# Re-pricing a static scheduler: new durations, a turn cost between 64 and 128 rows, and an offset per kind of step

## The chip, the cores and the metric

The kernel runs on one core of a Trainium2 chip. The metric is the device time of one execution in microseconds (us). Five engines work side by side, each through its own queue in program order: TensorE (PE, matmuls; its weight loads are PEld), VectorE (DVE), ScalarE (ACT), GpSimd (POOL), and SyncE (SP), which here issues all DMAs.

## The reference, cut to what matters

Linear attention with an exponential feature map, and then two MLPs over the same 2304 tokens, in 32-bit floats:

```python
def phi(x):                                   # x: 4 x 8 heads x 576 x 64
    proj = einsum('bhsd,df->bhsf', x, w_phi)  # f = 128
    proj = proj - max(abs(proj), axis=-1, keepdims=True)
    return concatenate([exp(proj), exp(-proj)], axis=-1)
q_p, k_p = phi(q), phi(k)
kv  = einsum('bhsf,bhsd->bhfd', k_p, v)
z   = sum(k_p, axis=2)
num = einsum('bhsf,bhfd->bhsd', q_p, kv)
den = einsum('bhsf,bhf->bhs', q_p, z)[..., None] + 1e-06
x   = (num / den) as 2304 x 512
x   = elu(x @ w_in) @ w_out                   # 512 -> 2048 -> 512
x   = (h * clip(h + 3, 0, 6) / 6) @ w2_out    # h = x @ w2_in
```

## The kernel before

The attention part is eight **units**, each of two heads over two batches. A unit is a set of steps, named by two letters and made by `add` in `unit` (from L250 on). In the order of their dependence they are:

- LD (SP): loads of raw k, q and v. Only unit 0 loads k and q in two pieces each (`LDk0`, `LDk1`, `LDq0`, `LDq1`).
- PJ (TensorE, L314): projections, matmuls of 64 rows, in three groups: all of k but the ninth block, the two ninth blocks ("x8"), all of q but the ninth block; unit 0 has five smaller groups. They write four banks of PSUM, the ring "p".
- MX and SB (DVE, L324 and L338): the largest absolute value, and the shift by it. SB releases the bank.
- EX (ACT, L347 and L354): both exponentials of k. KV (TensorE, L372): the sums of k times v, 72 matmuls of 128 rows and 130 columns in a unit, into the bank "a0" or "a1". ST (ACT, L390 and L392) copies them out.
- QT (TensorE, L397 and L403): transposes of shifted q into a bank of the ring "t", which has two. QE (ACT, L410 and L419): both exponentials of them. QT8 and QE8 are those of the ninth block.
- NM (TensorE, L431): numerator and denominator, into a bank of "t"; it needs ST and QE. NS (ACT, L446 and L450): copies of both out of the bank.
- RT, RV, RB (DVE, L455, L461, L469): transpose, reciprocal, transpose; MU (POOL, L478): the product, which is the MLPs' input.

A 32-bit matmul of the attention part stands in the trace as two instructions.

The MLP part works on groups of four 128-wide slices of the hidden layer over five blocks of tokens (four of 512 and one of 256). A step `hid` (L746) is 12 matmuls into a bank "p"; then come `act1` (ACT, L759, L760 or L762), `gate` (DVE, L773), `gate_hi` (ACT, L781), `gate_lo` (DVE, L788), and `outp` (L807), 12 matmuls into the banks "a0", "a1", "t0", "t1". Each 32-bit operand is split into a high and a low part, of which three products are taken. Weights come as 64-bit floats and are turned into 32-bit ones by eight integer steps on DVE (L675, L683, L687) and one on POOL (L692), and are split by two more on POOL (L714, L720). There are 32 weight pairs ("w"), each of two halves, in six slots. The first four slots exist from the start, so the weights of the first group are converted beside the attention part.

No order is written out. Every step states its engine, a duration, what it comes after (`after`: when that has ended; `behind`: when that has started), the buffers that it takes and a **rank**. `in_order` (L48) then plays the whole program through: at each turn it computes for each engine the soonest start of every ready step, keeps the steps within `WINDOW` of the soonest, and takes of these the one with the lowest rank. The queues of all engines, SP's and POOL's included, are issued in the order of the starts that it finds. A unit's step has the rank `u * PERIOD - tail`, where `tail` is the longest chain of durations from it to the unit's end. The MLP steps have the rank of a clock that starts at 8 times `PERIOD` and runs on by the matmuls' durations. A weight's steps have the rank of its first use less `W_LEAD`; in the first group they are spread over the units (`lead`).

Of the kernel before, what the change touches and what calls it, by code (L numbers as in the profile page):

```python
# [18 lines left out]
M1_GROUPS, M2_GROUPS = (4, 4, 4, 4), (4, 4, 4, 4)  # L19


PB, TB = 4, 2
KB, QB, KPB, EB, NSB, MXB, WB, GB = 3, 6, 3, 4, 2, 6, 4, 2
PERIOD, PROJ, TURN = 22.0, 0.225, 0.4
W_LEAD = 60.0


class Token:


    def __init__(self, ring):
        self.ring, self.users = ring, []


class Step:
    def __init__(self, engine, us, fn, after=(), rank=0.0, takes=(), uses=(), port=False, behind=()):
        self.engine, self.us, self.fn, self.rank, self.port = engine, us, fn, rank, port
        self.after, self.behind, self.takes = list(after), list(behind), list(takes)
        for t in uses:
            t.users.append(self)  # L40
        self.start = self.end = None


LATENCY = {"PE": 0.22, "DVE": 0.10, "ACT": 0.12, "POOL": 0.12, "SP": 2.2, "NONE": 0.0}
WINDOW = 0.06


def in_order(steps, rings):  # L48

    taken = {r: [] for r in rings}  # L50
    free = {e: 0.0 for e in LATENCY}
    port = 0.0
    waits, heirs = {}, {}
    for s in steps:
        need = {id(x): x for x in s.after + s.behind}
        waits[id(s)] = len(need)
        for x in need.values():
            heirs.setdefault(id(x), []).append(s)
    ready = {e: [s for s in steps if s.engine == e and not waits[id(s)]] for e in LATENCY}
    out = []  # L60

    def soonest(s):
        t = max([0.0] + [x.end + LATENCY[x.engine] for x in s.after] + [x.start for x in s.behind])
        extra = {}
        for k in s.takes:
            had = taken[k.ring]
            at = len(had) + extra.get(k.ring, 0) - rings[k.ring]
            extra[k.ring] = extra.get(k.ring, 0) + 1
            if at < 0:
                continue  # L70
            if at >= len(had):
                return None
            for x in had[at].users:
                if x.end is None:
                    return None
                t = max(t, x.end + LATENCY[x.engine])
        return t

    known = {}
    while len(out) < len(steps):  # L80
        best = None
        for e, some in ready.items():
            est = []
            for s in some:
                t = soonest(s)
                if t is not None:
                    t = max(t, free[e])
                    if s.port or e == "POOL":
                        t = max(t, port)
                    est.append((t, s))  # L90
            if est:
                t0 = min(t for t, _ in est)
                t, s = min(((t, s) for t, s in est if t <= t0 + WINDOW), key=lambda x: (x[1].rank, x[0]))
                if best is None or t < best[0]:
                    best = (t, s)
        if best is None:
            raise RuntimeError(f"no step can go on: {[(x.engine, x.rank, x.fn) for e in ready.values() for x in e][:40]}")
        t, s = best
        s.start, s.end = t, t + s.us
        if s.engine != "NONE":  # L100
            free[s.engine] = s.end
        if s.port or s.engine == "POOL":
            port = s.end
        for k in s.takes:
            taken[k.ring].append(k)
        ready[s.engine].remove(s)
        for x in heirs.get(id(s), ()):
            waits[id(x)] -= 1
            if not waits[id(x)]:
                ready[x.engine].append(x)  # L110
        out.append(s)
    order = sorted(range(len(out)), key=lambda i: (out[i].start, i))
    return [out[i] for i in order]
# [5 lines left out]


def pe1(n):
    return n / 2280 + 0.006


def dve(n):
# [1 line left out]


def act(n):
    return n / 1200 + 0.105  # L130


def pool(n, two=True):
# [4 lines left out]
def attention_then_two_mlps(  # L138
# [32 lines left out]
    R = S // 64  # L171
# [78 lines left out]
    def unit(u):  # L250
# [3 lines left out]
        def add(name, engine, us, fn, after=(), stage=None, **kw):  # L254

            s = step(engine, us, fn, after=[S_[x] for x in after], **kw)
            S_[name] = s
            if stage:
                s.behind += last.get((u - 1, stage), [])
                last.setdefault((u, stage), []).append(s)  # L260
            return s
# [22 lines left out]
        if u == 0:  # L284
            add("LDk0", "SP", 1.2, lambda: load("k", 0, 512), takes=[Tk["k"]], rank=-9)
            add("LDw", "SP", 0.6, lambda: nc.sync.dma_start(out=wphi, in_=w_phi), rank=-8)
            add("LDq0", "SP", 1.2, lambda: load("q", 0, 512), takes=[Tk["q"]], rank=-7)
            add("LDk1", "SP", 1.6, lambda: load("k", 512, R * 128), after=["LDk0"], rank=-6)
            add("LDq1", "SP", 1.6, lambda: load("q", 512, R * 128), after=["LDq0"], rank=-5)
            add("LDv", "SP", 1.6, load_v, takes=[Tk["v"]], rank=-4)  # L290
            ld = {("k", 0): ["LDk0", "LDw"], ("k", 1): ["LDk1"], ("q", 0): ["LDq0"], ("q", 1): ["LDq1"]}
        else:
            for s_ in "kq":
                add("LD" + s_, "SP", 2.8, bind_(load, s_, 0, R * 128), takes=[Tk[s_]], rank=(u - 1) * PERIOD, stage="LD")
            add("LDv", "SP", 1.6, load_v, takes=[Tk["v"]], rank=(u - 1) * PERIOD, stage="LD")
            ld = {(s_, i): ["LD" + s_] for s_ in "kq" for i in range(2)}
# [188 lines left out]
        for js in runs if u == 0 else (("k0", "k1"), ("x8",), ("q0", "q1")):  # L485
            items = [x for j in js for x in ITEMS[j]]
            tp = {(j, h): take("p") for j in js for h in range(2)}
            need = sorted({x for s_, r in items for x in ld[s_, int(r >= 4)]})
            pj = "PJ" + js[0]
            add(pj, "PE", len(items) * PROJ + TURN, bind_(projs, js), after=need, stage="PJ", takes=list(tp.values()),  # L490
                uses=[Tk[x] for x in sorted({s_ for s_, _ in items})])
            if js == ("x8",):
                Tk["sh8"] = take("sh8")
            for j in js:
                n = len(ITEMS[j]) * NF
                for h in range(2):
                    tm, ts = take("mx"), Tk["sh8"] if j == "x8" else take({"k": "shk", "q": "shq"}[j[0]])
                    add(f"MX{j}{h}", "DVE", dve(n), bind_(peak, j, h), after=[pj], takes=[tm],
                        uses=[tp[j, h]], stage="MX")
                    add(f"SB{j}{h}", "DVE", dve(n), bind_(shift, j, h), after=[f"MX{j}{h}"], stage="SB",  # L500
                        takes=[] if j == "x8" and h else [ts], uses=[tp[j, h], tm])
                    Tk["sh", j, h] = ts
# [18 lines left out]
                    S_[f"KV{j}{h}"].behind.append(S_[f"KVk0{h}"])  # L521
        for h in range(2):
            t = Tk["st", h] = take(f"st{h}")
            add(f"ST{h}", "ACT", act(260) + act(252), bind_(stat, h), after=[f"KV{j}{h}" for j in ("k0", "k1", "x8")],
                takes=[t], uses=[Tk["acc", h]], stage="ST")
        for c in range(2):
            for h in range(2):
# [1 line left out]
                Tk["e", h, c] = te  # L529
                add(f"QT{h}{c}", "PE", 4 * 0.109, bind_(q_tr, h, c), after=[f"SBq{c}{h}"], takes=[t],  # L530
                    uses=[Tk["sh", f"q{c}", h]], stage="QT")
                add(f"QE{h}{c}", "ACT", 2 * act(512), bind_(q_exp, h, c), after=[f"QT{h}{c}"], takes=[te],
                    uses=[t], stage="QE")
        t = take("t")
        add("QT8", "PE", 2 * 0.109, q_tr8, after=["SBx80", "SBx81"], takes=[t], uses=[Tk["sh8"]], stage="QT")
        add("QE8", "ACT", 4 * act(128), q_exp8, after=["QT8"], uses=[t], stage="QE")
        S_["QT8"].behind += [S_["QT01"], S_["QT11"]]
        S_["QE8"].behind += [S_["QE01"], S_["QE11"]]
        before = None
        for c in range(2):  # L540
            n = 64 * (4 + c)
            for bb in range(2):
                tn = take("nsd")
                for h in range(2):
# [1 line left out]
                    add(f"NM{h}{c}{bb}", "PE", 2 * pe4(n), bind_(num, h, c, bb),  # L546
                        after=[f"ST{h}", f"QE{h}{c}"] + ["QE8"] * c, takes=[t],
                        uses=[Tk["st", h], Tk["e", h, c]], stage="NM")
                    add(f"NS{h}{c}{bb}", "ACT", 2 * act(n) + 0.05, bind_(num_out, h, c, bb), after=[f"NM{h}{c}{bb}"],
                        takes=[tn] if h == 0 else [], uses=[t], stage="NS")  # L550
                    if before:
                        S_[f"NM{h}{c}{bb}"].behind.append(before)
# [14 lines left out]
            for x in s.after:  # L567
                tail[id(x)] = max(tail.get(id(x), 0.0), tail[id(s)] + LATENCY[x.engine])
        for s in mine:
            s.rank = u * PERIOD - tail[id(s)]  # L570
        for name, s in S_.items():
            (a_users if name[:2] in ("LD", "PJ", "MX", "SB", "EX", "KV") else b_users).append(s)
            if name[:2] == "SB":
# [272 lines left out]
    for w in range(2 * FT):  # L846
        j = w % len(SLOT)
        WT[w] = Token(f"w{j}")
        for i in range(2):
            lead = max(first[w] - W_LEAD, (2 * w + i + 1) * PERIOD / 1.2 if w < GROUPS[0][1] else 0.0)  # L850
            ts_, ta, tb = Token("s"), Token("ca"), Token("cb")
            x = step("SP", 1.4, bind_(fetch, w, i), takes=[ts_], rank=lead - 5, behind=[chain] if chain else [])
            chain = x
            cost = [0.6, 0.33, 0.33, 0.5, 0.6, 0.6, 0.6, 0.45]
            fns = to_f32(w, i)
            for n_, (us, fn) in enumerate(zip(cost, fns)):
                x = step(
# [150 lines left out]
```

## Time and profile before

| what | value |
|---|---|
| time, median of 3 runs | 1005.57 us (1004.29 to 1007.49) |
| profiled execution, time | 1007.1 us |
| its span in the trace | 1005.3 us |
| matmuls | 5312 |
| busy: TensorE, DVE, ACT, POOL | 986.8, 718.1, 422.7, 280.4 us |
| granted clock of TensorE, mean | 0.997 |

The span runs from the first to the last instruction of the profiled execution; its time holds 1.8 us more. Engines work at the same time, so the busy times don't add up to the span. Records of matmuls overlap each other by their pipelined ends: the distance between starts tells what a matmul costs, not its length.

### The profile page before, as it was taken

The page shows a single profiled execution, that of the slowest core. Times are in us where ns is not written, and L with a number is a line of the kernel's source. Part 1 is how long each engine was busy: PE and PEld are TensorE (multiplying, and loading weights), DVE is VectorE, ACT ScalarE, POOL GpSimd, SP SyncE. Part 2 cuts the span into 40 slices and gives each one's busy share as a digit, 9 for nine tenths or more (in the row PEclk, how much of TensorE's full clock was granted, in tenths as well). Part 3 has the DMA queues.
Part 4 walks back from the last instruction along what each step waited for, and adds up shares of the span by engine and source line. Part 5 has one row for each costly group of instructions (what it writes and reads, how often), then busy time and mean ns, then how long its engine had stood idle before and what let it go on. Part 6 is the DMA issues. An engine that isn't in the chain of part 4 may idle for free.

```text
span 1005.3 us, 13762 instructions
## 1 busy us (share of the span) xinstructions
PE 986.8 (98%) x5312; PEld 829.9 (83%) x5312; DVE 718.1 (71%) x1222; ACT 422.7 (42%) x815; POOL 280.4 (28%) x262
## 2 busy tenths in 40 slices
PE   8999999999999999999999999999999999999998
PEld 7878888877888888888887888888888888888886
DVE  4899999888227883888488958963996499734333
ACT  2777777874444333333334443433322222222222
POOL 2233442341005220531144545412431233130000
PEclk8999999999999999999999999999999999999999
DMA  8344442111001120112011100220121011000111
GB/s 215 93 113 114 115 117 62 43 43 38 6 1 30 55 74 11 43 42 84 1 43 42 63 22 22 70 78 1 43 84 42 1 43 63 21 1 35 49 42 64
DMA packets 33297, 53.44 MB, mean 53 GB/s; under 512 B 20304, under 2 KB 20432, under 8 KB 33232
## 3 DMA queue, kind: packets, MB, share of 16 engines
q1 hardware_dynamic: 33232, 52.57, 17.5%
q8 instruction: 42, 0.69, 0.3%
q14 instruction: 23, 0.19, 0.1%
HBM read 47.84 MB, written 4.72 MB: 52 GB/s over the span
## 4 chain that ended last, share of the span: by engine, by line
PE 91%; ACT 4%; DVE 4%; issue 0%; POOL 0%; POOLq 0%; ACTq 0%
PE ps_p L746 37%; PE ps_a L807 20%; PE ps_t L807 18%; PE ps_a L372 7%; PE ps_t L431 5%; PE ps_p L314 3%; ACT e L410 1%; PE ps_t L397 1%; DVE xl L731 1%; DVE gl L788 1%; ACT kp L347 1%; ACT e L419 1%; ACT nd L446 1%; DVE x L820 0%; ACT ns L450 0%
## 5 line engine op out<-in xcount | busy, mean ns | idle before, releaser
L773 DVE SCALAR_TENSOR_TENSOR g<-e,ps_p 128x512 f32<-128x512 f32 (+1 forms) x160 | 101.1, 632 | 187.4 <-ACT e L762 110.7
L746 PE MATMUL ps_p<-xh,w_h 128*128 128x512 f32 (+1 forms) x512 | 185.7, 363 | 0.0
L746 PE MATMUL ps_p<-xh,w_l 128*128 128x512 f32 (+1 forms) x512 | 185.6, 362 | 0.0
L746 PE MATMUL ps_p<-xl,w_h 128*128 128x512 f32 (+1 forms) x512 | 185.6, 362 | 0.0
L692 POOL TENSOR_TENSOR w_b<-w_b,w 128x512 int32<-128x512 int32 x64 | 88.6, 1384 | 292.5 <-DVE w L683 287.4
L788 DVE TENSOR_TENSOR gl<-g,gh 128x512 fp32r<-128x512 f32 (+1 forms) x160 | 124.5, 778 | 50.5 <-ACT gh L781 47.6
L781 ACT CAST gh<-g 128x512 fp32r<-128x512 f32 (+1 forms) x160 | 93.0, 581 | 123.1 <-DVE g L773 120.0
L762 ACT ACTIVATE e<-ps_p,half_c 128x512 f32<-128x512 f32 (+1 forms) x80 | 51.7, 646 | 220.4 <-PE ps_p L746 220.4
L759 ACT ACTIVATE e<-ps_p 128x512 f32<-128x512 f32 (+1 forms) x80 | 44.5, 556 | 167.9 <-PE ps_p L746 167.9
L746 PEld LDWEIGHTS ps_p<-xh,w_h 128*128 128x128 f32 x512 | 96.6, 189 | 16.0
L746 PEld LDWEIGHTS ps_p<-xl,w_h 128*128 128x128 f32 x512 | 96.5, 189 | 15.9
L746 PEld LDWEIGHTS ps_p<-xh,w_l 128*128 128x128 f32 x512 | 96.6, 189 | 15.0
L714 POOL TENSOR_SCALAR w_h<-w_b 128x512 fp32r<-128x512 f32 x64 | 45.5, 711 | 189.0 <-PE ps_t L807 101.0
L687 DVE SCALAR_TENSOR_TENSOR w_b<-w,w_b 128x512 int32<-128x512 int32 x128 | 90.9, 710 | 2.5
L683 DVE TENSOR_SCALAR w_a<-w_a 128x512 int32<-128x512 int32 x128 | 89.0, 695 | 1.4
L720 POOL TENSOR_TENSOR w_l<-w_b,w_h 128x512 fp32r<-128x512 f32 x64 | 87.0, 1360 | 5.1
L431 PE MATMUL ps_t<-e,st 128*128 128x256 f32 (+1 forms) x256 | 70.9, 419 | 4.4 <-ACT e L410 2.3
L372 PEld LDWEIGHTS ps_a<-vb,kp 128*128 128x128 f32 x576 | 69.0, 195 | 1.8 <-issue 0.2
L372 PE MATMUL ps_a<-vb,kp 128*128 128x130 f32 x576 | 70.2, 279 | 0.0
L807 PE MATMUL ps_a<-w_h,gl 128*128 128x512 f32 x160 | 62.6, 391 | 0.7 <-DVE gl L788 0.6
L807 PE MATMUL ps_a<-w_h,gh 128*128 128x512 f32 x160 | 62.6, 391 | 0.1
L431 PEld LDWEIGHTS ps_t<-e,st 128*128 128x128 f32 x256 | 44.9, 189 | 21.6 <-ACT ns L450 5.7
(90 smaller groups left out, 1914.1 us busy)
## 6 DMA issues: line engine op xcount, KB each, us to landing
w<-in_moe_w_in_dram SPq DMA_DIRECT2D x32, 512.0 KB, 3.4
w<-in_moe_w_out_dram SPq DMA_DIRECT2D x32, 512.0 KB, 3.4
vb<-in_v_dram SPq DMA_DIRECT2D x16, 288.0 KB, 5.4
out_dram<-x SPq DMA_DIRECT2D x18, 256.0 KB, 2.1
raw_k<-in_k_dram SPq DMA_DIRECT2D x7, 576.0 KB, 3.7
raw_q<-in_q_dram SPq DMA_DIRECT2D x7, 576.0 KB, 4.0
raw_k<-in_k_dram SPq DMA_DIRECT2D x1, 320.0 KB, 5.4
raw_q<-in_q_dram SPq DMA_DIRECT2D x1, 320.0 KB, 5.0
```

The lines of the kernel that those rows point to most:

```text
L372: nc.tensor.matmul(out=acc[h][:, half].rearrange("p b d -> p (b d)"), lhsT=kp[:, i, half, :], rhs=vb[u % 2][:, r].rearrange("p h c -> p (h ...
L431: nc.tensor.matmul(out=ps[:, :n], lhsT=ST[h][:, half * 2 + bb, :], rhs=e[:, o:o + n], start=(half == 0), stop=(half == 1),)
L683: V.tensor_scalar(out=st[o], in0=st[x], scalar1=s1, scalar2=s2, op0=o1, **kw)
L687: return lambda: V.scalar_tensor_tensor(out=st["b"], in0=st[x], scalar=s1, in1=st["b"], op0=o1, op1=ALU.bitwise_or)
L692: nc.gpsimd.tensor_tensor(out=st["b"], in0=st["b"], in1=st["l"], op=ALU.add)
L720: nc.gpsimd.tensor_tensor(out=lo[:, i], in0=F.pop((w, i)), in1=hi[:, i].bitcast(F32), op=ALU.subtract)
L746: nc.tensor.matmul(out=ps[:, :n], lhsT=a_[:, 0, c], rhs=x_[kk], start=(i == 0), stop=(i == 3 * KD - 1),)
L762: nc.scalar.activation(out=e[:, :n], in_=ps[:, :n], func=AF.Relu, scale=1.0 / 6.0, bias=half_c)
L773: V.scalar_tensor_tensor(out=gt[:, :n], in0=e[:, :n], scalar=s, in1=ps[:, :n], op0=o0, op1=o1)
L781: nc.scalar.copy(out=gh[:, :n], in_=G[m, b, f][:, :n])
L788: V.tensor_tensor(out=gl[:, :n], in0=gt[:, :n], in1=gh[:, :n].bitcast(F32), op=ALU.subtract)
L807: nc.tensor.matmul(out=o, lhsT=a_, rhs=b_, start=(fi == 0 and i == 0), stop=(fi == fn - 1 and i == 2))
```

## The change

Only numbers and dependences of the scheduler change; no instruction is added, removed or reshaped.

- PERIOD, PROJ, TURN, WINDOW, LATENCY and `W_LEAD` get new values. `TURN` is no longer part of each PJ's duration; it is added to a TensorE step's start when the step before it had another number of rows (`rows`, 64 for PJ, else 128).
- `BIAS` adds an offset to the rank of each kind of step of a unit, `W_BIAS` to the rank of the first group's weights.
- The durations of ST, QE, QE8, NS, of matmuls (`pe1`), of ACT (`act`) and of the eight weight steps on DVE get new values.
- In unit 0 the loads are chained by start: k0, (w_phi,) q0, k1, q1, v. Before, k1 came after the landing of k0, q1 after that of q0, and v was free.

```diff
-PERIOD, PROJ, TURN = 22.0, 0.225, 0.4
-W_LEAD = 60.0
+PERIOD, PROJ, TURN = 27.5, 0.22, 0.19
+BIAS = {
+    "LD": 60.6, "ST": 49.7, "MU": -38.2, "QE": 2.0, "RB": -60.2,
+    "RV": 68.6, "PJ": -20.3, "NM": -25.9, "KV": 3.0, "QT": -4.7,
+    "MX": 46.7, "EX": 29.7, "NS": 5.9, "RT": -36.0, "SB": 10.8,
+}
+W_LEAD, W_BIAS = 21.4, 113.0
...
-LATENCY = {"PE": 0.22, "DVE": 0.10, "ACT": 0.12, "POOL": 0.12, "SP": 2.2, "NONE": 0.0}
-WINDOW = 0.06
+LATENCY = {"PE": 0.25, "DVE": 0.11, "ACT": 0.14, "POOL": 0.12, "SP": 2.2, "NONE": 0.0}
+WINDOW = 0.2
...
-                    t = max(t, free[e])
+                    t = max(t, free[e] + (TURN if e == "PE" and s.rows != rows else 0.0))
...
+        if s.engine == "PE":
+            rows = s.rows
...
-    return n / 2280 + 0.006
+    return n / 2392 + 0.013
...
-    return n / 1200 + 0.105
+    return n / 1200 + 0.095
...
-            add("LDk1", "SP", 1.6, lambda: load("k", 512, R * 128), after=["LDk0"], rank=-6)
-            add("LDq1", "SP", 1.6, lambda: load("q", 512, R * 128), after=["LDq0"], rank=-5)
-            add("LDv", "SP", 1.6, load_v, takes=[Tk["v"]], rank=-4)
+            add("LDk1", "SP", 1.6, lambda: load("k", 512, R * 128), behind=[S_["LDq0"]], rank=-6)
+            add("LDq1", "SP", 1.6, lambda: load("q", 512, R * 128), behind=[S_["LDk1"]], rank=-5)
+            add("LDv", "SP", 1.6, load_v, takes=[Tk["v"]], rank=-4, behind=[S_["LDq1"]])
...
-            add(pj, "PE", len(items) * PROJ + TURN, bind_(projs, js), after=need, stage="PJ", takes=list(tp.values()),
+            add(pj, "PE", len(items) * PROJ, bind_(projs, js), after=need, stage="PJ", takes=list(tp.values()), rows=64,
...
-            add(f"ST{h}", "ACT", act(260) + act(252), bind_(stat, h), after=[f"KV{j}{h}" for j in ("k0", "k1", "x8")],
+            add(f"ST{h}", "ACT", 0.715, bind_(stat, h), after=[f"KV{j}{h}" for j in ("k0", "k1", "x8")],
...
-                add(f"QE{h}{c}", "ACT", 2 * act(512), bind_(q_exp, h, c), after=[f"QT{h}{c}"], takes=[te],
+                add(f"QE{h}{c}", "ACT", 0.96, bind_(q_exp, h, c), after=[f"QT{h}{c}"], takes=[te],
...
-        add("QE8", "ACT", 4 * act(128), q_exp8, after=["QT8"], uses=[t], stage="QE")
+        add("QE8", "ACT", 0.63, q_exp8, after=["QT8"], uses=[t], stage="QE")
...
-                    add(f"NS{h}{c}{bb}", "ACT", 2 * act(n) + 0.05, bind_(num_out, h, c, bb), after=[f"NM{h}{c}{bb}"],
+                    add(f"NS{h}{c}{bb}", "ACT", 2 * act(n) + 0.22, bind_(num_out, h, c, bb), after=[f"NM{h}{c}{bb}"],
...
-            s.rank = u * PERIOD - tail[id(s)]
+            s.rank = u * PERIOD - tail[id(s)] + BIAS.get(s.kind, 0.0)
...
-            lead = max(first[w] - W_LEAD, (2 * w + i + 1) * PERIOD / 1.2 if w < GROUPS[0][1] else 0.0)
+            lead = max(first[w] - W_LEAD, (2 * w + i + 1) * PERIOD / 1.2 + W_BIAS if w < GROUPS[0][1] else 0.0)
...
-            cost = [0.6, 0.33, 0.33, 0.5, 0.6, 0.6, 0.6, 0.45]
+            cost = [0.34, 0.34, 0.34, 0.34, 0.62, 0.62, 0.62, 0.34]
```

## Rows read from the trace of the kernel before

**Rows 1.** The page: each engine's busy us, share of the span, instructions.

```profile
PE 986.8 (98%) x5312; PEld 829.9 (83%) x5312; DVE 718.1 (71%) x1222; ACT 422.7 (42%) x815; POOL 280.4 (28%) x262
```

**Rows 2.** Table of stretches: us, busy PE, PEld, DVE, ACT, POOL, granted clock, DMA.

```profile
0.00:25.35 25.35, 21.11 (x169) 19.92 (x169) 11.17 (x20) 7.73 (x14) 5.45 (x18) 0.87 0.80 213
...
75.00:99.52 24.52, 23.62 (x196) 20.05 (x195) 22.76 (x49) 18.40 (x43) 9.91 (x10) 1.00 0.46 117
...
250.00:985.00 735.00, 733.13 (x3473) 615.52 (x3472) 497.23 (x788) 244.03 (x421) 201.21 (x172) 1.00 0.12 39
```

**Rows 3.** Timeline of TensorE, one unit: start, us, what, [idle before, releaser].

```profile
75.00 2.06 PE L314 MATMUL ps_p<-wphi,raw_k 64*128 64x128 f32 x32
...
77.26 0.60 PE L397 MATMUL ps_t<-ident,shq 128*128 128x128 f32 x4
78.30 0.66 PE L397 MATMUL ps_t<-ident,shq 128*128 128x128 f32 x4 [0.44 <-ACT e L419]
79.27 2.11 PE L431 MATMUL ps_t<-e,st 128*128 128x256 f32 x8 [0.32 <-ACT e L410]
81.32 0.49 PE L314 MATMUL ps_p<-wphi,raw_k 64*128 64x128 f32 x4
...
82.17 2.02 PE L431 MATMUL ps_t<-e,st 128*128 128x256 f32 x8
...
92.30 5.52 PE L372 MATMUL ps_a<-vb,kp 128*128 128x130 f32 x48
97.65 1.04 PE L397 MATMUL ps_t<-ident,shq 128*128 128x128 f32 x8
98.53 1.06 PE L372 MATMUL ps_a<-vb,kp 128*128 128x130 f32 x8
```

**Rows 4.** Timeline of ACT, the same unit.

```profile
78.10 2.10 ACT L410 ACTIVATE e<-ps_t 128x512 f32<-128x512 f32 x4
80.01 1.21 ACT L347 ACTIVATE kp<-shk 128x512 f32<-128x512 f32 x2
81.25 0.47 ACT L446 ACTIVATE nd<-ps_t,eps_c 64x256 f32<-64x256 f32 x1
...
82.14 0.47 ACT L446 ACTIVATE nd<-ps_t,eps_c 64x256 f32<-64x256 f32 x1
...
98.29 1.57 ACT L410 ACTIVATE e<-ps_t 128x512 f32<-128x512 f32 x3 [4.83 <-PE ps_t L397]
```

**Rows 5.** Weight lines on DVE, 25 to 197 us: ns min/median/max, first and last start.

```profile
L683 DVE TENSOR_SCALAR w_a<-w_a x24: 384/424/1409, 34.7 to 179.2; 128x512 int32<-128x512 int32 x24
...
L687 DVE SCALAR_TENSOR_TENSOR w_b<-w,w_b x24: 649/691/1637, 37.3 to 184.7; 128x512 int32<-128x512 int32 x24
```

**Rows 6.** Timeline of all engines, the first 30 us.

```profile
1.65 0.42 SPq L272 DMA_DIRECT2D raw_q<-in_q_dram  x1
...
3.42 1.50 SPq L276 DMA_DIRECT2D vb<-in_v_dram  x2
...
4.96 1.21 SPq L272 DMA_DIRECT2D raw_k<-in_k_dram  x1
...
6.62 1.06 PE L314 MATMUL ps_p<-wphi,raw_q 64*128 64x128 f32 x16
...
8.02 1.28 DVE L338 TENSOR_TENSOR shk<-ps_p,mx 128x512 f32<-128x512 f32 x2
...
10.54 2.17 PE L314 MATMUL ps_p<-wphi,raw_k 64*128 64x128 f32 x16 [2.87 <-DVE mx L324]
```

**Rows 7.** The page's DMA issues: KB each, median us from issue to landing.

```profile
raw_k<-in_k_dram SPq DMA_DIRECT2D x1, 320.0 KB, 5.4
```

**Rows 8.** Waits, 222 to 985 us: who for whom, us in total, times, longest.

```profile
POOL w_h L714 <- PE ps_t L807: 101.0, 4, 51.6
...
PE ps_a L807 <- DVE gl L788: 2.4, 3, 1.1
```

**Rows 9.** Waits, 197 to 250 us.

```profile
PE ps_t L431 <- ACT ns L450: 0.6, 2, 0.4
```

More of the change, by code (lines that the diff above doesn't have):

```diff
@@ L35, with __init__ @@
 class Step:
-    def __init__(self, engine, us, fn, after=(), rank=0.0, takes=(), uses=(), port=False, behind=()):
-        self.engine, self.us, self.fn, self.rank, self.port = engine, us, fn, rank, port
+    def __init__(self, engine, us, fn, after=(), rank=0.0, takes=(), uses=(), port=False, behind=(), rows=128):
+        self.engine, self.us, self.fn, self.rank, self.port, self.rows = engine, us, fn, rank, port, rows
         self.after, self.behind, self.takes = list(after), list(behind), list(takes)
@@ L51, in in_order @@
     free = {e: 0.0 for e in LATENCY}
-    port = 0.0
+    port, rows = 0.0, 128
     waits, heirs = {}, {}
@@ L256, in add @@
             s = step(engine, us, fn, after=[S_[x] for x in after], **kw)
-            S_[name] = s
+            S_[name], s.kind = s, name[:2]
             if stage:
```

## Prediction

> **What bounds the kernel now.** I read the page's busy shares first: TensorE is busy in nearly the whole span and no other engine comes near it [rows 1]. The table of stretches then says where the rest is lost [rows 2]: a first stretch of 25.35 us that is slower and partly at the lower clock (mean granted 0.87), one attention unit of 24.52 us in the steady state (TensorE 23.62 busy), the passage to the MLPs, and the 735 us of MLP with 733.13 us busy. So the MLP part, nearly three quarters of the span, has at most some 2 us to give, and the kernel can get faster only in the first 220 us. Nothing in the arithmetic changes: 5312 matmuls remain, at the same shapes.
>
> A busy TensorE hides short stalls, because its records overlap. I therefore read the timeline of one unit by starts [rows 3]. The 32 matmuls of PJ from 75.00 to the transposes' start cost about 0.062 each; four transposes cost 0.44 (a x8 group of them, 97.65 to 98.53, lasts 0.88). Against that: QT at 77.26 should be over at 77.70, but the next QT starts at 78.30, waiting for ACT (the QE8 exponentials): 0.60 lost. That QT is over at 78.74, but NM starts at 79.27, again waiting for ACT (QE): 0.53 lost. The small PJ at 81.32 has 8 matmuls, 0.50, but NM follows at 82.17: 0.35 lost, part of which is the turn between 64 and 128 rows. Together 1.48 us of 24.52. The same three gaps, within 0.03 us, stand in each of the seven stretches of this length between 25.35 and 197.44 (in the second of them the third gap is 0.6 longer).
>
> The ACT rows say why [rows 4]: ACT sat idle for 4.83 us until 98.29, while TensorE ran 48 matmuls of KV without a break from 92.30 on [rows 3], and then everything (QE, ST, QE8, QE) arrives together, and TensorE waits behind it. ACT isn't short of time over a unit (18.40 of 24.52 busy [rows 2]); its work is in the wrong place. That is a fault of order, and order is what the change edits.
>
> **The change part by part.**
>
> Durations. These numbers enter nothing but the scheduler, so each costs nothing by itself; what matters is whether they are nearer to the trace. The ACT rows [rows 4]: four exponentials from 78.10 to 80.01, so 0.955 for the two of one QE (old price 1.063, new 0.96). One NS (two copies) from 81.25 to 82.14: 0.89 (old 0.687, new 0.837). The old prices thus charged QE too much and NS a fifth too little, which is how a plan could look free of stalls and meet three on the chip. I take the new ones as closer on ACT. On DVE the weight conversion goes from 4.01 to 3.56 us per half weight, while the rows give medians of 424 and 691 ns [rows 5]: 5 x 0.42 + 3 x 0.69 = 4.2 us by duration. Part of each duration overlaps the next instruction, so 3.56 is a floor without contention; here the new plan may be too hopeful by 0.6 us per half.
>
> TURN. Each PJ paid 0.4 in its own duration; now a change of rows costs 0.19 in each direction, 0.38 for a PJ between other steps. The number of PJ steps stays (three in a unit) and the four "p" banks force SB between them. I take zero. Bounds: nothing, to two turns fewer per unit at half of 0.35 us [rows 3], 2 x 0.18 x 8 = 2.8 us gained; a loss would need more PJ steps, and there are none.
>
> Offsets (BIAS) and PERIOD. By the ranks, with the old tails of a few us behind each kind, the old TensorE order of preference was PJ, KV, QT, NM of a unit, then the next unit. The new offsets (NM -25.9, PJ -20.3, QT -4.7, KV +3.0, period 27.5) make it NM, QT, PJ of the next unit, and KV about last. KV needs no evacuation per bank, so it becomes the filler, and QT is offered to TensorE ahead of it. That addresses the 4.83 us in which ACT had nothing: QT can go between pieces of KV. If QT and QE move earlier by 2 us, the waits of 0.60 and 0.53 go, for ACT has 24.52 - 18.40 = 6.1 us of slack in the unit [rows 2]. What is late next is ST and the first NM (see rivals). On DVE, RT and RB go first and the weights, 113 us later in rank, behind the early units. I take 70% of the seams: 7 x 1.48 x 0.7 = 7.3 us. Bounds: nothing, to 7 x 1.48 = 10.4 us.
>
> First loads. The last halves of k and q now go ahead of v on SP's queue. Before, v stood third; it was issued only at 3.42, 1.35 us after the issue before it was over, for its buffer was still being cleared by POOL, and the second half of k was queued behind it until 4.96 [rows 6]. That load took 5.4 us to land, so 10.4 [rows 7], and TensorE, through with q at 7.7, starts on it at 10.54 (the row names DVE, whose release of the bank was earlier: SB of k0 is over at 8.02 + 1.28 = 9.30 [rows 6]). Issued at about 2.1 it lands by about 7.5 (up to 9 if the transfers crowd each other), and the bank at 9.30 is late next: TensorE starts at about 9.45, 1.1 us earlier. v is queued behind two issues of 0.4 us, both over before 3.42, so it is issued no later; it may land later behind 640 KB, by 2 to 3 us, and KV would start at 12 instead of 12.6. I take 1.0 us gained, bounds -0.5 to 2 (the first stretch has a mean granted clock of 0.87 [rows 2], and if TensorE is busy without a break earlier, its rise may come earlier too). All other loads keep 10 us and more of lead; I price them at zero, and at the 5.4 us of that landing each time that the lead is gone.
>
> Weights. W_LEAD falls from 60 to 21.4. In the MLP part this binds little: POOL's splitting waits 101.0 us in all (longest 51.6) for TensorE to release a weight's slot [rows 8], so weights stand ready long before use. TensorE's waits for gl, the low half of the gate, are 2.4 us in all, three times; a DVE queue less burdened with early weights gets some of it. I take 0.5, bounds -3 to 2. In the passage to the MLPs TensorE waits 0.6 for ACT's NS [rows 9]; with NS priced right I take 0.4, bounds 0 to 0.6.
>
> Sum: 7.3 + 0 + 1.0 + 0.5 + 0.4 = 9.2 us. The profiled span of 1005.3 would become 996.1. The profiled execution took 1007.1 us, 1.8 more than its span; the median of the three runs is 1005.57, so I take the difference from the median: 996.4.
>
> **A rule that speaks against it.** The worst of 24 short weight operations on DVE took 1409 ns against a median of 424 [rows 5], so some of them are held up. The Trainium skill, page "SBUF — State Buffer", section "SBUF: two separate sides", says that DVE and GpSimd share a port pair under an exclusive lock, and that the loser waits for the other's whole instruction. It is the mechanism that I would put behind that row, and its effect is the third rival below.
>
> **The rivals.**
>
> Same: the stalls move instead of going. Two "t" banks serve all transposes and NM, and each is released by ACT; if QT comes earlier, NM's banks come later. For it: every wait in the unit is for ACT. Against: the 6.1 us of slack. With three quarters of the 10.4 us back in other places, 2.6 us, and 0.5 from the loads, the time is 1002.5 to 1006.
>
> Slower: KV as filler exposes ST. ST needs all KV of its unit, NM needs ST. Now PJ of the next unit (1.98 us at 75.00 [rows 3]) stands between the last KV and NM and hides ST; in the new order that PJ may be spent before KV ends. Uncovered, a unit pays ST's two heads, 0.715 each by the diff, plus a signal each way, together some 1.8 us. Seven units cost 12.6 against 10.4 + 1.0 gained if all else goes well; in the likelier case of 7.3 + 1.0 it is 4.3 us slower: 1010. It decides from 1.2 us uncovered per unit on. Against it: the scheduler knows this chain and its prices are near the rows.
>
> DVE as the bound: a unit has 22.76 us of DVE [rows 2], of which two half weights are about 8.4, so a unit shortened to 23.1 has 0.3 us to spare. With one collision of 1409 - 424 = 1.0 us per unit [rows 5] the unit stays at 23.8, gaining 7 x 0.7 = 5 at most, with the loads 6: 999.5. Against: only eight half weights are needed before the MLPs, and by rank the rest may wait.
>
> **How the numbers follow.** Forecast (988 to 1001, centre 996.4): 0.60. DVE bound (998 to 1002): 0.12. Same: 0.16. Slower by ST: 0.12. A measurement of this kernel tells about 0.3%, 3 us, from no change. Faster takes the forecast and most of the DVE case: 0.71; same 0.16; slower 0.13. The range leaves out the ST case and a little of the low end: the full sum of upper bounds, 10.4 + 2.8 + 2 + 2 + 0.6 = 17.8, would be 988, which needs everything at once, so 990; up to 1005.5 for the case of no change.
>
> **What would show it.** In the profile after: a steady unit of 23.3 to 23.8 us by starts instead of 24.52; no wait of TensorE for the exponentials of QE8 and QE; ACT's idle 4.83 us before QE broken into smaller pieces; QT between pieces of KV; the second half of k issued before v and TensorE's 2.87 us wait at 10.54 down to about 1.8; an MLP stretch as long as before. Wrong would be: units of 24.5 us with the waits at ST or "t" banks, TensorE waiting for DVE's SB, or a gap ahead of the first hidden matmuls for want of weights.

## The result

The changed kernel took 993.88 us (median; 992.83 to 996.28) against 1005.01 us of the kernel before beside it: a ratio of 0.9888, 95% interval 0.9862 to 0.9915. A second measurement of the same kernel (`e12_after_again` below) gave 993.71 and 0.988 (0.9863 to 0.9896). The profiled execution took 992.83 us with a span of 991.0; that of before had 1005.3. The lines of the changed kernel stand 8 lower in the code (L372 is L380, and so on).

The page of the changed kernel, busy shares (before: [rows 1]):

```profile
PE 980.2 (99%) x5312; PEld 829.4 (84%) x5312; DVE 740.3 (75%) x1222; ACT 421.1 (42%) x815; POOL 282.0 (28%) x262
```

Its table of stretches (before: [rows 2]; columns as there). The second and third rows are two units in the steady state, the last is an MLP stretch that starts and ends about 14 us earlier than the one of before:

```profile
0.00:25.35 25.35, 21.06 (x203) 19.48 (x203) 14.96 (x26) 11.28 (x23) 5.45 (x18) 1.00 0.92 233
75.45:98.38 22.93, 22.93 (x195) 20.20 (x195) 21.72 (x43) 18.48 (x44) 7.20 (x8) 1.00 0.40 99
98.38:121.31 22.93, 22.93 (x197) 20.20 (x195) 21.17 (x41) 18.15 (x43) 8.55 (x10) 1.00 0.41 104
236.60:970.70 734.10, 732.68 (x3471) 615.16 (x3470) 518.91 (x817) 243.40 (x421) 208.20 (x177) 1.00 0.12 41
```

A steady unit went from 24.52 to 22.93 us, and TensorE has no idle time left in it. The first row's granted clock went from 0.87 to 1.00 in these two executions; other executions of both kernels differ in it (last section). The timeline of TensorE in one such unit (before: [rows 3]):

```profile
96.39 2.06 PE L322 MATMUL ps_p<-wphi,raw_q 64*128 64x128 f32 x32
98.38 1.99 PE L439 MATMUL ps_t<-e,st 128*128 128x256 f32 x8
100.21 1.95 PE L380 MATMUL ps_a<-vb,kp 128*128 128x130 f32 x16
101.99 1.89 PE L439 MATMUL ps_t<-e,st 128*128 128x256 f32 x8
103.72 1.95 PE L380 MATMUL ps_a<-vb,kp 128*128 128x130 f32 x16
105.51 2.32 PE L439 MATMUL ps_t<-e,st 128*128 128x320 f32 x8
107.75 0.49 PE L322 MATMUL ps_p<-wphi,raw_k 64*128 64x128 f32 x4
108.08 0.39 PE L322 MATMUL ps_p<-wphi,raw_q 64*128 64x128 f32 x4
108.40 2.42 PE L439 MATMUL ps_t<-e,st 128*128 128x320 f32 x8
110.75 2.06 PE L322 MATMUL ps_p<-wphi,raw_k 64*128 64x128 f32 x32
112.74 1.09 PE L405 MATMUL ps_t<-ident,shq 128*128 128x128 f32 x8
113.67 1.95 PE L380 MATMUL ps_a<-vb,kp 128*128 128x130 f32 x16
115.45 0.38 PE L411 MATMUL ps_t<-ident,sh 128*128 128x128 f32 x2
115.67 0.60 PE L405 MATMUL ps_t<-ident,shq 128*128 128x128 f32 x4
116.11 1.95 PE L380 MATMUL ps_a<-vb,kp 128*128 128x130 f32 x16
117.90 0.60 PE L405 MATMUL ps_t<-ident,shq 128*128 128x128 f32 x4
118.33 1.06 PE L380 MATMUL ps_a<-vb,kp 128*128 128x130 f32 x8
119.32 2.06 PE L322 MATMUL ps_p<-wphi,raw_q 64*128 64x128 f32 x32
```

No row has an idle time. The block of 48 KV matmuls is cut into pieces of 8 and 16, with QT and NM between them. Each QT follows its PJ of q by some 16 us (96.39 to 112.74) instead of 9.6 (88.05 to 97.65 before). ACT's longest idle time in this unit is 1.67 us, where it was 4.83 [rows 4]; its timeline, the row after that gap, and the exponentials of two QE:

```profile
106.79 0.52 ACT L454 ACTIVATE nd<-ps_t,eps_c 64x320 f32<-64x320 f32 x1 [1.67 <-PE ps_t L439]
...
113.43 2.06 ACT L418 ACTIVATE e<-ps_t 128x512 f32<-128x512 f32 x4 [0.86 <-PE ps_t L405]
```

The first 13 us of TensorE (before: [rows 6]):

```profile
6.51 1.06 PE L322 MATMUL ps_p<-wphi,raw_q 64*128 64x128 f32 x16
8.23 0.46 PE L322 MATMUL ps_p<-wphi,raw_k 64*128 64x128 f32 x2 [0.66 <-DVE shk L346]
9.60 1.13 PE L322 MATMUL ps_p<-wphi,raw_k 64*128 64x128 f32 x14 [0.91 <-DVE shk L346]
10.83 0.66 PE L405 MATMUL ps_t<-ident,shq 128*128 128x128 f32 x4
12.73 3.81 PE L380 MATMUL ps_a<-vb,kp 128*128 128x130 f32 x32 [1.24 <-ACT e L418]
```

Where the time went, by the two profiled spans (14.3 us apart; the medians are 11.1 apart). From the first NM of unit 0 to the first NM of unit 7 it took 29.63 to 204.12 before and 26.87 to 191.78 now: 174.49 and 164.91, 9.6 us less. Up to that first NM 2.8 less. From unit 7's first NM to the end, the passage and the MLPs, 801.2 and 799.3: 1.9 less. The gain in the medians is not one of the clock: the executions of either kernel whose mean granted clock was 1.000 took 992.53 and 992.89 us now, and 1003.87 and 1004.18 before.

### The profile page after: what moved, and what is told of

Read it like the earlier page. It is cut to its first block, busy times and chain, and to the rows that moved or that the text cites. A ratio compares the mean times of both kernels' runs of the same rounds, so it can differ in the third digit from the quotient of the medians.

```text
span 991.0 us, 13774 instructions
## 1 busy us (share of the span) xinstructions
PE 980.2 (99%) x5312; PEld 829.4 (84%) x5312; DVE 740.3 (75%) x1222; ACT 421.1 (42%) x815; POOL 282.0 (28%) x262
## 4 chain that ended last, share of the span: by engine, by line
PE 89%; DVE 9%; ACT 2%; issue 1%; POOL 0%; DVEq 0%; POOLq 0%; ACTq 0%
PE ps_p L754 38%; PE ps_a L815 20%; PE ps_t L815 18%; PE ps_t L439 5%; PE ps_a L380 4%; PE ps_p L322 2%; DVE mx L332 1%; PE ps_t L405 1%; DVE gl L796 1%; DVE w_b L695 1%; DVE shk L346 1%; DVE shq L346 1%; DVE x L828 1%; DVE g L781 1%; DVE w_a L691 0%
## 5 line engine op out<-in xcount | busy, mean ns | idle before, releaser
L700 POOL TENSOR_TENSOR w_b<-w_b,w 128x512 int32<-128x512 int32 x64 | 91.2, 1425 | 312.8 <-DVE w L691 312.8
L691 DVE TENSOR_SCALAR w_a<-w_a 128x512 int32<-128x512 int32 x128 | 100.7, 787 | 1.6
L380 PE MATMUL ps_a<-vb,kp 128*128 128x130 f32 x576 | 70.9, 275 | 1.2 <-ACT e L418 1.2
L380 PEld LDWEIGHTS ps_a<-vb,kp 128*128 128x128 f32 x576 | 68.6, 191 | 2.7 <-issue 1.4
L815 PE MATMUL ps_a<-w_l,gh 128*128 128x512 f32 x160 | 62.5, 390 | 0.0
```

The costliest lines, as they stand in the source:

```text
L380: nc.tensor.matmul(out=acc[h][:, half].rearrange("p b d -> p (b d)"), lhsT=kp[:, i, half, :], rhs=vb[u % 2][:, r].rearrange("p h c -> p (h ...
L691: V.tensor_scalar(out=st[o], in0=st[x], scalar1=s1, scalar2=s2, op0=o1, **kw)
L700: nc.gpsimd.tensor_tensor(out=st["b"], in0=st["b"], in1=st["l"], op=ALU.add)
L815: nc.tensor.matmul(out=o, lhsT=a_, rhs=b_, start=(fi == 0 and i == 0), stop=(fi == fn - 1 and i == 2))
```

## The experiments

Each is one kernel against the kernel before on the same chip. A unit is counted from the first NM of one unit to that of the next. In the order below they are called e1 (prices alone), e2 (offsets alone), e3 (loads alone), e4 (KV first), e8 and e9 (the window), e7 (TensorE's offsets), e5 (weight ranks), e11 (the turn's price), e6 (old loads), e12 (the changed kernel again) and e10 (old loads with idle work).

**Prices alone.** The changed kernel with its new durations, but with the old ranks, window, weight leads and loads:

```diff
-PERIOD, PROJ, TURN = 27.5, 0.22, 0.19
-BIAS = { ... }
-W_LEAD, W_BIAS = 21.4, 113.0
-WINDOW = 0.2
+PERIOD, PROJ, TURN = 22.0, 0.22, 0.19
+BIAS = {}
+W_LEAD, W_BIAS = 60.0, 0.0
+WINDOW = 0.06
```

> The kernel before with the new durations, signal times and the turn cost by rows, but with no offsets, the old period (22), window (0.06), weight leads and load order. Theory A (the offsets make the order): TensorE still takes KV in one block and then the transposes, so a steady unit stays at 24.0 to 24.6 us by starts and the time at 1001 to 1006. Theory B (wrong prices were the fault, and right ones suffice): the three gaps of 1.48 us per unit go, a unit is below 23.3 us, and the time is 994 to 998.

1046.63 us, ratio 1.0391 (1.0371 to 1.0412): neither theory, 40 us slower, 30 to 31.6 us per unit. Its TensorE timeline, and a row of its table of stretches:

```profile
39.45 5.52 PE L376 MATMUL ps_a<-vb,kp 128*128 128x130 f32 x48
44.91 2.06 PE L318 MATMUL ps_p<-wphi,raw_q 64*128 64x128 f32 x32
50.33 1.34 PE L401 MATMUL ps_t<-ident,shq 128*128 128x128 f32 x8 [3.37 <-DVE shq L342]
```

```profile
51.40:58.10 6.70, 6.38 (x34) 5.54 (x33) 6.63 (x15) 4.34 (x13) 1.84 (x2) 0.50 0.55 161
```

Here KV is spent before PJ of q, not behind it as at 88.05 to 92.30 in the kernel before. DVE needs some 5 us for the four maxima and the four shifts (47.11 to 51.98 in its own timeline), nothing is left to cover them, TensorE waits 3.37 us, and then its granted clock is at 0.50, the lower of its two levels, for 6.7 us. This comes again in every unit; it is the fault that the old order did not have.

**Offsets alone.** The kernel before with BIAS, period, window and weight leads of the change, but old durations and old loads (the other half of the change).

> The kernel before with the new offsets, period, window and weight leads, but with the old durations, signal times and turn cost, and the old load order. Theory A: the order is that of the ranks, so units of 23.0 to 23.6 us and a time of 994 to 998, whatever the prices. Theory B: with NS priced a fifth too low the plan meets waits for ACT again, units of 23.8 to 24.5 us, 999 to 1005. A third reading, that offsets and durations were fitted to each other: slower than either alone, over 1005.

1001.83 us, ratio 0.9955 (0.994 to 0.997): some two fifths of the gain of the whole, in the time that theory B gives. But the units are 24.6 us, no better than before. The waits for QE are gone, with QT ahead of the block of 48 KV matmuls; in their place TensorE waits in nearly every unit for ACT's ST, and NM stands in one block of 32 matmuls, which takes 8.91 us by starts instead of 8.15 in the changed kernel, where KV stands between its pieces:

```profile
75.51 8.98 PE L436 MATMUL ps_t<-e,st 128*128 128x256 f32 x32 [0.46 <-ACT st L397]
```

What is gained lies at the two ends: the first NM comes at 25.92 instead of 29.63, and from unit 6's first NM to the end it takes 825.2 instead of 828.0. A part of the first is the clock, which did not fall in this execution.

**Loads alone.** The kernel before with the three lines of unit 0's loads.

> The kernel before with only the new order of unit 0's loads (q and k second halves ahead of v). Theory of the prediction: the second half of k lands by 7.5 to 9 us, the wait of 2.87 us at 10.54 shrinks by 1.1, and the time falls by about 1.0 us to 1003.5 to 1004.5. Rival (the clock): if the shorter wait keeps TensorE's granted clock at full speed in the stretch from 9.8 to 16.6 us, where it was at half, some 3 us more are gained: 1000.5 to 1002. Rival (v late): KV starts later than 12.64 and nothing is gained.

1007.37 us, ratio 1.0007 (0.9996 to 1.0018): no gain, as the rival of the late v has it; KV starts at 12.81. Its first three units take 25.0 to 25.2 us (before 24.5 to 25.1), the later ones 24.52 as before. The equal medians seem to hide two effects that cancel. Executions with the same mean granted clock are slower than those of the kernel before: 1004.47 to 1005.45 against 1004.18 us at 1.000, 1008.06 to 1008.57 against 1006.77 to 1007.67 at 0.996. But three of its ten executions had 1.000, and one of the thirteen beside it.

**KV first.** The changed kernel with one number turned:

```diff
-    "RV": 68.6, "PJ": -20.3, "NM": -25.9, "KV": 3.0, "QT": -4.7,
+    "RV": 68.6, "PJ": -20.3, "NM": -25.9, "KV": -40.0, "QT": -4.7,
```

> The changed kernel with one number turned: KV's offset from +3 to -40, so that KV goes ahead of QT and PJ again. Theory (KV as filler, with QT between its pieces, is what empties the gaps): KV stands in blocks of 40 and more matmuls again, ACT idles for over 2 us in a unit, the waits for QE come back, units of 23.8 to 24.6 us, time 998 to 1005. Rival (the offset of KV matters little, since what is ready when decides): units stay at 22.9 to 23.2 us and the time within 2 us of 993.9.

1045.59 us, ratio 1.0387 (1.0369 to 1.0406). That KV must stand behind PJ of q holds, far beyond the time expected, but the wait is not the one that I had named: TensorE waits for the shift of q on DVE (22.1 us in all), as in the first experiment. KV ahead of QT but behind PJ was not tried, so this run says nothing of QT between the pieces of KV.

**The window.** The first experiment with the new window, and the changed kernel with the old one:

```diff
-WINDOW = 0.06
+WINDOW = 0.2
```

> New durations without offsets as in e1_durations, but with the new window of 0.2 in place of 0.06 (old period, weight leads and loads). What failed there was seen in its trace: KV is spent before PJ of q, and TensorE then waits 3.3 us per unit for DVE's shift of q, and its clock falls. Theory F (filter): PJ now starts 0.19 later than its rivals in the plan, and with a window of 0.06 it is never a candidate while any 128-row step is ready; at 0.2 it is, so the waits for shq go, units of 23.0 to 24.6 us, time 994 to 1006. Rival R (rank): without offsets KV of a unit outranks PJ of the next anyway, so KV still goes first, units near 30 us, time 1035 to 1050.

> The changed kernel with the old window, 0.06 in place of 0.2, and nothing else. Theory F (filter): PJ falls out of the candidates again whatever its offset, KV is spent first, TensorE waits for shq, units of 28 to 31 us, time 1030 to 1050. Rival R (rank): the offsets hold the order, units of 22.9 to 24 us, time 993 to 1000.

1011.98 us, ratio 1.0053 (1.0038 to 1.0068), with units of 24.82; and 1042.03 us, ratio 1.0339 (1.0314 to 1.0365), with units of 29.0 to 29.9. Theory F holds in both, though the first is 6 us over its range and its units a little over theirs. A turn of 0.19 is added to PJ's soonest start in the plan; with a window of 0.06 PJ drops out of the candidates while any step of 128 rows can start at once, and no offset can bring it back, for ranks are compared among candidates alone. So some 34 of the 40 us of the first experiment were the turn's price beside the old window. The window of 0.2 is just wider than the turn. With it, the first experiment is rid of the waits for DVE, and the waits for ACT of the kernel before are what is left. The TensorE timeline of e8_dur_window, and below it that of e9_window_old:

```profile
103.19 4.19 PE L435 MATMUL ps_t<-e,st 128*128 128x256 f32 x16 [0.45 <-ACT e L414]
...
108.31 2.42 PE L435 MATMUL ps_t<-e,st 128*128 128x320 f32 x8 [0.28 <-ACT ns L454]
```

```profile
77.18 2.06 PE L322 MATMUL ps_p<-wphi,raw_q 64*128 64x128 f32 x32
81.43 1.23 PE L405 MATMUL ps_t<-ident,shq 128*128 128x128 f32 x8 [2.19 <-DVE shq L346]
```

**Offsets of TensorE's steps alone.** The changed kernel with

```diff
+BIAS = {"PJ": -20.3, "NM": -25.9, "KV": 3.0, "QT": -4.7}
```

> The changed kernel with the offsets of TensorE's steps alone (PJ, NM, KV, QT); those of loads, DVE, ACT and POOL are zero. Theory (the order on TensorE makes the gain): units of 22.9 to 23.5 us, time 993 to 998. Rival (each engine's queue must fit the others, as the weight ranks alone cost 8 us): TensorE waits for shq or for ST again, units over 24 us, time over 1000.

1003.88 us, ratio 0.9972 (0.9963 to 0.9982), units of 24.3 to 24.6. My theory fell and the rival holds: the offsets of TensorE's steps do not do it alone. QT stands between pieces of KV here too and no wait for QE is left. The wait is the one of the prediction's "slower" rival, ST without cover, once per unit; TensorE's timeline:

```profile
101.62 1.06 PE L376 MATMUL ps_a<-vb,kp 128*128 128x130 f32 x8
103.67 1.99 PE L435 MATMUL ps_t<-e,st 128*128 128x256 f32 x8 [0.98 <-ACT st L396]
```

**Weight ranks.** The changed kernel with `W_LEAD, W_BIAS = 60.0, 0.0`.

> The changed kernel with the old weight ranks (lead 60, no offset for the first group). Theory of the prediction: the weights in the MLP part wait for slots, not for rank, so the MLP part is within 1 us; in the attention part the weights go ahead of MX and SB again and the early units get up to 1 us longer: 994 to 1000. Rival (the weight ranks matter as much as the offsets): DVE is late with the shift of q, TensorE waits for it, units over 24 us and a time over 1003.

1001.8 us, ratio 0.9953 (0.9938 to 0.9968), 8 us over the changed kernel and above the theory's range. Up to the first NM this execution is 2.4 us later, with the clock at 0.50 for 3.4 us from 14.3 on, which that of the changed kernel had not. From there to unit 4's first NM the units are as there (four take 93.9 us, there 94.4), and from the last NM to the end, the MLPs, it is 783.5 against 784.3. Most of the loss, 8.2 us, lies between, in the last units and the passage, where NM waits for ST and not, as the rival had it, for the shift of q:

```profile
148.23 1.99 PE L439 MATMUL ps_t<-e,st 128*128 128x256 f32 x8 [2.18 <-ACT st L400]
...
204.70 1.99 PE L439 MATMUL ps_t<-e,st 128*128 128x256 f32 x8 [1.38 <-ACT st L400]
```

**The turn's price.** The changed kernel with `TURN = 0.0`.

> The changed kernel with the turn between 64 and 128 rows priced at 0 instead of 0.19 in the plan. By the prediction the turn's price is worth nothing by itself (as many turns as before): 992 to 996. Rival (a plan fitted to its prices breaks when one is altered, whichever it is): stalls of another kind come up, 998 to 1010.

1001.46 us, ratio 0.995 (0.9932 to 0.9968), 7.6 us over the changed kernel, with units between 22.4 and 26.4 us and the last at 32.0 (24.6 in the changed kernel). The rival holds. Up to the first NM this execution is 2.6 us later than that of the changed kernel, with the clock at 0.50 from 10.4 on (last section); later NM waits for ST twice:

```profile
173.40 3.04 PE L439 MATMUL ps_t<-e,st 128*128 128x256 f32 x8 [1.88 <-ACT st L400]
205.36 0.92 PE L439 MATMUL ps_t<-e,st 128*128 128x256 f32 x3 [1.87 <-ACT st L400]
```

**Old loads, and the clock.** The changed kernel with the old order of unit 0's loads; the changed kernel unaltered; and the old loads with idle work on TensorE:

```diff
             for j in js:
                 proj(j)
+            if u == 0 and js == ("q0",):
+                for _ in range(16):
+                    nc.tensor.transpose(warm[:, 0:128], ident, ident)
```

> The changed kernel with the old order of unit 0's loads. Theory: the order of loads is worth about 1 us or less (e3_loads, which had it alone, had the median of the kernel before), time 993.5 to 996. Rival (clock): its worth is that TensorE is not idle for 2.9 us at the start, so that its clock does not fall; here that wait comes back, the granted clock is at half for some 6.8 us near 10 to 17 us, and the time is 996 to 998.

> The changed kernel once more, unaltered, beside the next one. Its time should be 993 to 995 again. The old order of loads (e6_loads_old) gave 991.98: if loads in the new order truly cost time, this stays 1.5 to 2 us above that; if the difference came from where TensorE's clock fell in each run, the two overlap.

> The changed kernel with the old order of unit 0's loads and, right behind PJ of q in unit 0, 16 more transposes of the identity into the bank that the warm-up uses, whose result nobody reads: TensorE works through the 2.24 us in which it waits for v. Theory (a wait of over 2 us lets the clock fall, and 3.4 us at half speed cost some 1.7): no fall between 8 and 17 us in the trace, 1 to 2 us less than e6_loads_old, 990 to 991. Rival (the fall does not hang on that wait): the fall stays, and the time is 991.5 to 993, or over it by up to 1.7 us if the transposes run at half speed and hold back KV.

991.98 us, ratio 0.9854 (0.984 to 0.9869); 993.71 us, 0.988 (0.9863 to 0.9896); 991.16 us, 0.985 (0.9835 to 0.9864). The old loads are 1.7 to 1.9 us ahead of the new ones in the medians, where both theories of e6 had them level or behind; their interval and those of the changed kernel overlap by less than 0.001. At a mean granted clock of 1.000 it is 991.17 against 992.53 and 992.89, at 0.998 it is 992.79 and 992.98 against 994.53 and 994.73: the same difference, of few executions (one of the changed kernel, 993.02 us at 0.997, does not fit). The clock is seen in the tables of stretches of the two kernels with old loads, without the added transposes and with them:

```profile
10.00:12.00 2.00, 1.61 (x9) 1.64 (x10) 1.93 (x4) 1.01 (x2) 0.00 (x0) 0.69 1.04 421
12.00:14.00 2.00, 2.00 (x11) 1.77 (x12) 0.47 (x1) 0.00 (x0) 0.00 (x0) 0.50 1.12 339
```

```profile
10.00:12.00 2.00, 1.53 (x14) 1.56 (x15) 1.39 (x3) 0.00 (x0) 0.00 (x0) 1.00 1.04 423
12.00:14.00 2.00, 2.00 (x33) 1.88 (x33) 0.39 (x1) 0.00 (x0) 0.00 (x0) 1.00 1.09 360
```

With the transposes the clock does not fall, and the first NM comes at 26.47 instead of 28.00. That part of the theory holds in the trace, and all four executions with the transposes had a mean granted clock of 1.000, where those without had 1.000, 0.999, 0.998 and 0.998. In the median it is 0.8 us, and the intervals overlap, so the gain in time is not settled. This kernel is the fastest of the study: its interval ends at 0.9864, and that of the changed kernel run beside it begins at 0.9863.

## Why the prediction was right, and where it was not

The direction, the place and nearly the size came out: 9.2 us forecast off the median, 11.1 measured, most of it in the attention part. That the sum is so near is partly luck: the seams and the passage gave more than their terms, and the loads, booked as a gain, cost time.

**The seams.** This is the term that was too small: seven units gave 9.6 us instead of 7.3. Four of them are steady and lost 1.59 each. The first two, at 24.07 and 24.51 between first NMs, hold 32 more matmuls of PJ than before, and the last (24.61 against 26.75) 32 fewer, so the three have to be taken together: 3.2 us. Of the three gaps the waits of 0.60 and 0.53 are gone. The third was not all to be had: from the small PJ to NM it is now 0.65 (107.75 to 108.40) instead of 0.85, and some 0.15 over the 0.50 of its matmuls remains, which I take for the turn. Another 0.25 comes from where the prediction had nothing: the 32 matmuls of NM take 8.15 us by starts instead of 8.40. The rows for it were there: ACT had 6.1 us of slack in a unit, and 1.13 of the 1.48 us were waits for it. The mechanism, KV as filler with QT between its pieces, is in the timeline, and it goes with the waits for QE: they are gone where QT stands between pieces of KV or ahead of them (the changed kernel, e2, e7), and they are there where QT stands behind a block of 48 (the kernel before, e8). No run turned this alone. But I gave KV's place one reason, ACT's work spread over the unit. It has a second and dearer one (e1, e4, e9), which I did not see because the old order satisfied it: KV covers the 5 us that DVE takes between PJ of q and QT, and putting it ahead of PJ costs 52 us.

**"These numbers enter nothing but the scheduler, so each costs nothing by itself."** True of the instructions and wrong as a guide to the time. New prices without the rest cost 40 us (6 with the new window), the turn's price at zero 7.6 us, the old window 48 us. I priced the turn at nothing because the number of turns stays; that number wasn't the point. In this scheduler the turn's price decides who is a candidate, and WINDOW and TURN must be read together, which the prediction did not do at all.

**First loads, 1.0 us.** This step failed. k's second half was issued at 2.12 and TensorE did begin on it at 8.23, but the wait was only cut in pieces: 0.66 + 0.91 + 1.24 = 2.81 us against 2.87 [rows 6]. v was the price. The first of its two transfers was issued at 3.42 as before, yet behind 640 KB; the rows on its load are those of before and then of the changed kernel:

```profile
DMA to landing us min/median/max: 4.3/5.0/5.7
```

```profile
DMA to landing us min/median/max: 7.0/7.7/8.5
```

The second, issued at 4.11, landed at 12.6 by that 8.5 us. So KV starts at 12.73 (before 12.64; the row in the result names ACT, but what came last was v), where the old loads let it start at 10.39 in the new order. I had put v's delay at 2 to 3 us, which is what it is, and then let KV start at 12 all the same. The profiled executions of before and after differ by the fall of the clock from 9.8 to 16.6 us of the one, and the largest part of the 2.8 us up to the first NM is this; it may account for much of the 3.2 us by which the spans differ more than the medians. Whether the new order of loads keeps the clock up more often is not shown: five of the eight executions of the changed kernel had a mean of 0.997 or 0.998, and two of the four with the old loads.

**Weights.** In the MLP part the term was about right: from the last NM to the end it took 1.4 us less (forecast 0.5), and TensorE's waits for gl went from 2.4 to 1.1 us [rows 8], and the waits of POOL's splitting for a slot stayed long:

```profile
POOL w_h L722 <- PE ps_a L815: 74.9, 3, 25.0
POOL w_h L722 <- PE ps_t L815: 73.5, 3, 24.5
...
PE ps_a L815 <- DVE gl L796: 1.1, 1, 1.1
```

In the attention part the rank of the weights is worth 8 us, and I had no term for it there. In the passage TensorE's waits for NS, a term of 0.4, went from 0.6 us [rows 9] to none, and 0.3 for ST came in their place.

**The rivals.** "Slower by ST" did not come in this kernel: TensorE's waits for ST are 0.6 us in all from 25 to 190 us. But it is the very wait that comes up in e2, e5, e7 and e11, where a piece of the fit is missing. "DVE as the bound" did not decide: DVE is at 21.2 to 21.7 of 22.93 us, close, but TensorE is full. No run here priced the shared port that the prediction named as the mechanism behind it. "Same" did not come, as the 6.1 us of ACT's slack had said.

**What stays open.** Which of the eleven offsets off TensorE matters was not tried one by one; e7 takes all away at once. Nor is it shown by what steps a weight rank or a turn's price ends in a wait for ST; the waits are shown, the chain of choices behind them is not.

## What to carry to other kernels

The parts of a change to a greedy static scheduler don't add: here 40 us lost by prices alone and 3 to 5 gained by offsets alone make 11 gained together, and altering one piece of the whole (the window, the turn's price, KV's offset, the weight ranks, the offsets off TensorE) cost 8 to 52 us; only the loads could be taken back, with a gain of 1.7 to 1.9. So price such a change by the stalls that the trace shows it can remove, as the unit's timeline did here, and treat the plan as one piece that is measured whole. When a cost is added to one kind of step, compare it at once with the window or threshold that picks the candidates; and when a filler is moved, ask for every wait that it covered, the ones that the trace does not show included.

## What the runs showed of the hardware

TensorE's granted clock stood at 1.00 or at 0.50 (2.4 and 1.2 GHz), and each stretch at 0.50 before the end of a kernel begins in idle time of TensorE or shortly behind it: 6.8 us of it with a wait of 2.87 us in the kernel before, 3.4 with one of 2.24 in e6_loads_old, 6.8 with each of the seven waits of 3.26 to 3.41 us in e1_durations. The Trainium skill, "TensorE: Matmul & The Clock Gate", section "What's actually happening", says that an idle array falls back to the half rate; the traces agree. By an estimate from the e1_durations rows, 6.8 us at half speed cost 3.4 us, as much again as the wait; its units are some 6.2 us longer than 24.52.

What wait is enough the runs do not tell. The changed kernel's 2.81 us in three pieces were not followed by a fall, but in e11_no_turn, where the first two of these waits were as long, the clock was at 0.50 for 6.8 us from 10.4 on:

```profile
8.60 0.46 PE L322 MATMUL ps_p<-wphi,raw_k 64*128 64x128 f32 x2 [0.65 <-DVE shk L346]
9.97 1.69 PE L322 MATMUL ps_p<-wphi,raw_k 64*128 64x128 f32 x14 [0.91 <-DVE shk L346]
```

```profile
10.40:17.20 6.80, 5.86 (x32) 5.26 (x29) 4.67 (x8) 2.73 (x6) 0.00 (x0) 0.50 1.17 242
```

One wait of 2.06 us at the start of e2_offsets and one of 2.87 in the MLP part of e9_window_old were followed by none. Nor does the fall come in every execution of a kernel: the mean granted clock of the kernel before went from 0.996 to 1.000 over 33 executions beside the experiments. At 0.996 they took 1006.77 to 1007.69 us (twelve), at 1.000 they took 1003.87 and 1004.18. So one trace does not show whether a kernel keeps its clock, and some 3 us between two executions of one kernel can be the clock. With sixteen transposes whose result nobody reads all four executions kept it.

The queue of loads is paid in landing times: 640 KB put ahead of v moved the landing of its two transfers from 5.0 to 7.7 us after issue (medians), with the first issue at the same 3.42 us.
